# Moving the low-part subtracts of an attention and expert kernel from GpSimd to VectorE

## The chip, the cores and the metric

The kernel runs on one core of a Trainium2 chip. A core has TensorE (PE, matrix multiplies and transposes), VectorE (DVE), ScalarE (ACT), GpSimd (POOL) and a queue engine that only issues transfers (SyncE, SP). Each engine works through its own row of instructions in order, and waits on semaphores for the others. The metric is the device time of one execution in microseconds (us); lower is better.

## The reference, cut to what matters

```python
scores = q @ k.T / sqrt(64) + bias          # 4 batches x 8 heads, 576 x 576
attn = softmax(scores)                      # bias: a small network of the distance
x = (attn @ v) gathered to 2304 x 512
h = x @ w_in                                # 512 x 2048
g = h * tanh(log(1 + exp(h)))               # "mish"
out = g @ w_out                             # 2048 x 512
```

All in float32. The kernel multiplies in a rounded float32 format (F32R) and keeps accuracy by splitting an operand into a high part (the rounded value) and a low part (what the rounding left, value minus high part): three products, high by high, low by high and high by low, stand for one.

## The kernel before, in words

Three stages follow one another. The first (to about 55 us) makes the bias of all heads and writes it to DRAM. The second, attention, works through 16 pairs of heads (4 head pairs times 4 batches). The third is the expert part: two matrix multiplies with the gate between them.

A pair of heads in attention is five steps, one for each block of 128 query rows in the order `ORDER = [0, 1, 4, 2, 3]`; block 4 holds the last 64 rows of both heads, so that step has one score tile and the other four have two. `step(n)` writes a step out by hand, and its order is the order on every engine:

- `scores(n)` (L204): PE multiplies q and k, high and low parts, into score tiles `s`. There are two buffers of `s`, one for each head of a step.
- `add_bias(n)` (L216, one instruction pair at L227 for each head): DVE adds the bias from PSUM into `pt` and takes the row's extreme `m`. This frees `s`.
- `exps(n, 0)` and later `exps(n, 1)` (L232): ACT exponentials of the two heads.
- `transposes(n - 2)` (L272): PE transposes the weights of two steps ago into `tp`, ACT copies them out (`main`, `tail`, L286 to L305). In the second step of a pair the reciprocals of the sums go through here too, and DVE copies them out as `rt` (L254) once ACT has copied `tail`.
- `ahead(n)` (L362): issues loads for later pairs: `load_hi` on POOL's queue (the transfer that rounds to F32R), `load_raw` on SP's (the unrounded q and k, then v).
- `split(n)` (L381): `split_qk` makes the low part `qklo` of the next pair, and one of four parts of a weight's conversion runs: `scale_high`, `shift_low`, `merge`, then `sign` with `split_weights`. A weight so takes four steps, and 16 of them are converted in attention. `split_weights` lets ACT cast the weight to its high part (`whi` or `who`, L143), and an engine given as an argument subtracts (`wli` or `wlo`, L144).
- `pv_duo` (L307): PE multiplies weights and values into the only `o` buffer, in pieces that are spread over steps; DVE copies a finished `o` out as `x` (L325), in the second and fourth step. PE starts the next `o` in the third and fifth step, behind the transposes.

In the prediction steps are called first to fifth: block 0, 1, 4, 2, 3.

Of the kernel before, what the change touches and what calls it, by code (L numbers as in the profile page):

```python
# [7 lines left out]
F32 = mybir.dt.float32  # L8
F32R = mybir.dt.float32r
U32 = mybir.dt.uint32  # L10
AF = mybir.ActivationFunctionType
ALU = mybir.AluOpType
# [3 lines left out]
B, H, S, D, C = 4, 8, 576, 64, 32  # L16
# [3 lines left out]
P = 128  # L20
SH = S // 2
QW = 1280
# [22 lines left out]
def kernel(ctx: ExitStack, tc, qk, v, wb, w2, w_in, w_out, psia, psi4, rinv, eye, out):  # L45
    nc = tc.nc
    pe, dve, act, pool, sp = nc.tensor, nc.vector, nc.scalar, nc.gpsimd, nc.sync
# [57 lines left out]
    def scale_high(eng):  # L105

        job, w = w64.pop(0)
        high = convp.tile([P, 512], F32, name="high", bufs=1)  # L110
        if eng is act:
            act.mul(high, w.bitcast(F32)[:, :, 1], 2.0 ** -112)
        else:
            dve.tensor_scalar(high, w.bitcast(F32)[:, :, 1], 2.0 ** -112, None, op0=ALU.mult)
        half.append((job, w, high))
# [15 lines left out]
    def sign():  # L131
        job, high, c = half.pop(0)
        cu = c.bitcast(U32)
        dve.scalar_tensor_tensor(cu, high.bitcast(U32), 0x80000000, cu,
                                 op0=ALU.bitwise_and, op1=ALU.bitwise_or)
        w32.append((job, c))

    def split_weights(eng):
        job, c = w32.pop(0)
        if job not in w_hi:  # L140
            w_hi[job] = ring.tile([P, 512], F32R, name="wh{}{}{}".format(*job))
            w_lo[job] = ring.tile([P, 512], F32R, name="wl{}{}{}".format(*job))
        act.copy(w_hi[job], c)  # L143
        eng.tensor_tensor(w_lo[job], c, w_hi[job].bitcast(F32), op=ALU.subtract)  # L144
# [11 lines left out]
    hip = rsbuf("hip", 2, side="right")  # L156
# [3 lines left out]
    qk_raw, qk_hi, qk_lo, v_t, bias_t = {}, {}, {}, {}, {}  # L160
    st.tile([P, 32], F32, name="fill", bufs=1)

    def load_raw(i):
        hp, b = divmod(i, B)
        raw = rawp.tile([P, QW], F32, name="rawqk")
        sp.dma_start(out=raw, in_=qk[b, hp])
        vt = vp.tile([P, 2, 5, D], F32, name="vt")
        sp.dma_start(out=vt, in_=v[b, hp].rearrange("p (h c d) -> p h c d", h=2, c=5))
        qk_raw[i], v_t[i] = raw, vt

    def load_hi(i):
        hp, b = divmod(i, B)
        hi = hip.tile([P, QW], F32R, name="qkhi")
        pool.dma_start(out=hi, in_=qk[b, hp])
        qk_hi[i] = hi

    def split_qk(i):

        lo = hip.tile([P, QW], F32R, name="qklo")
        (pool if i else dve).tensor_tensor(lo, qk_raw.pop(i), qk_hi[i].bitcast(F32), op=ALU.subtract)  # L180
        qk_lo[i] = lo

    def load_bias(hp, c):
        h0, h1 = 2 * hp, 2 * hp + 1
        rows = P if c < 4 else 64
        src = bias_d[c][:, :rows * PITCH].rearrange("h (i j) -> h i j", j=PITCH)[:, :, PAD:PAD + S]
        t = bias_t[hp, c] = biasp.tile([P, 2 * S if c < 4 else 640], F32, name=f"bias{c}")[:, :2 * S if c < 4 else S]
        if c < 4:
            sp.dma_start(out=t[:, 0:S], in_=src[h0])
            sp.dma_start(out=t[:, S + 64:], in_=src[h1, :, 0:512])  # L190
            sp.dma_start(out=t[:, S:S + 64], in_=src[h1, :, 512:S])
        else:
            for r in range(2):
                sp.dma_start(out=t[r * 64:r * 64 + 64], in_=src[h0 + r])

    NPAIR = B * HP
# [141 lines left out]
    def load_x(blk, p):  # L338
        t0, n = blocks[blk]
        raw = p.tile([P, HP, TB], F32, name="xraw", bufs=1)  # L340
        for off, m, b, s in _x_runs(t0, n):
            sp.dma_start(out=raw[:, :, off:off + m], in_=x_d[b][:, :, s:s + m])
        x_raw[blk] = raw

    def load_r(blk, r, h0, h1):

        t0, n = blocks[blk]
        for off, m, b, s in _x_runs(t0, n):
            while m:
                k = min(m, 512 - s) if s < 512 else m  # L350
                for u in range(2):
                    if s < 512:
                        src = r_d[b][h0:h1, 4 * u:4 * u + 4].rearrange("p c j -> p (c j)")[:, s:s + k]
                    else:
                        src = r_d[b][h0:h1, 8, 64 * u + s - 512:64 * u + s - 512 + k]
                    sp.dma_start(out=r[64 * u:64 * u + 64, :, off:off + k],
                                 in_=src.unsqueeze(0).to_broadcast([64, h1 - h0, k]))
                off, m, s = off + k, m - k, s + k

    parts = []  # L360

    def ahead(n):  # L362

        i, x = divmod(n, 5)
        if x == 4 and i + 2 < NPAIR:
            load_hi(i + 2)
            load_raw(i + 2)
        if i % B == B - 1 and i // B + 1 < HP:
            load_bias(i // B + 1, ORDER[x])
        if n == NS - 11:  # L370
            load_x(0, x0)
        if n in (NS - 10, NS - 6):
            x_r[0] = x0.tile([P, 2, TB], F32, name="xr", bufs=1)
            h0 = 0 if n == NS - 10 else 2
            load_r(0, x_r[0], h0, h0 + 2)
        if n in (NS - 7, NS - 3):
            h0 = 0 if n == NS - 7 else 2
            for d in range(2):
                pool.tensor_tensor(x_raw[0][:, h0 + d], x_raw[0][:, h0 + d], x_r[0][:, d], op=ALU.mult)

    def split(n):  # L381

        i, x = divmod(n, 5)
        if (x == 1 or n == 3) and i + 1 < NPAIR:
            split_qk(i + 1)
        if half:
            parts.pop(0)()
        elif n > 5 and w64[0][0] in order[:HALF]:
            scale_high(act if x == 2 else dve)
            parts.extend((shift_low, merge, lambda: (sign(), split_weights(pool))))  # L390

    def step(n):
        i, x = divmod(n, 5)
# [63 lines left out]
    def reach(t):  # L457

        left, right = 16 * t + 15, S - 16 * t
        n = max(left + 1, right)  # L460
        return left, right, n + n % 2
# [12 lines left out]
    for idx in range(NB + 2):  # L474
# [4 lines left out]
        if idx + 2 < NB:  # L479
            n = reach(ts[idx + 2])[2]  # L480
# [6 lines left out]
    def make_h(idx):  # L487
        if idx >= NB:
            return
        n = reach(ts[idx])[2]  # L490
        for cg in range(4):
            e = maker[idx, cg]
            ht = ring.tile([P, 640], F32, name="ht")
            k = 4 * ts[idx] + cg
            if e == "a":
                act.activation(ht[:, :n], at[:, :n], AF.Relu, bias=bb[:, k:k + 1])
            else:
                dve.tensor_scalar(ht[:, :n], at[:, :n], bb[:, k:k + 1], 0.0, op0=ALU.add, op1=ALU.max)
            h_t[idx, cg] = ht

    def mirrored(idx):
        t = ts[idx]
        left, right, _ = reach(t)
        ps = bps_t[idx] = bps.tile([P, 1024], F32, name="bps")
        for a, b in ((0, min(left, 512)), (512, left), (left, 512), (max(left, 512), NW)):
            for cg in range(4 if a < b else 0):
                h = h_t[idx, cg]
                src = h[:, a - left:b - left] if a >= left else h[:, left - a:left - b:-1]
                pe.matmul(ps[cg * 32:cg * 32 + 32, a:b], w2t, src, start=True, stop=True)  # L509

    def evac(idx):
        t = ts[idx]
        bt = bo.tile([P, NW], F32, name="bt")
        if maker["out", idx] == "a":
            act.mul(bt, bps_t.pop(idx)[:, :NW], rinv_t[:, t:t + 1])
        else:
            dve.tensor_scalar(bt, bps_t.pop(idx)[:, :NW], rinv_t[:, t:t + 1], None, op0=ALU.mult)

        c = t // 8
        a = (16 * t - P * c) * PITCH + PAD - 15  # L520
        dst = bias_d[c][:, a:a + 16 * (PITCH + 1)].rearrange("h (i j) -> i h j", j=PITCH + 1)
        sp.dma_start(out=dst[:, :, :NW], in_=bt)
# [5 lines left out]
    for idx in range(NB + 2):  # L528
        if idx < NB:
            make_h(idx + 2)  # L530
            mirrored(idx)
        if 1 <= idx <= NB:
            evac(idx - 1)
        if idx == 1:
            load_raw(0)
        if idx == 12:
            split_qk(0)
        if idx in BIAS_AT:
            load_bias(0, ORDER[BIAS_AT.index(idx)])
        for lag, do in enumerate((scores, add_bias, exps)):  # L540
            if idx - lag in SOFT_AT:
                for u in range(2 if lag == 2 else 1):
                    do(SOFT_AT.index(idx - lag), *((u,) if lag == 2 else ()))
        if idx == 33:
            load_hi(1)
        if idx == NB:
            load_raw(1)
        if idx == NB + 1:
            load_weights()
    bias_scope.close()  # L550
# [259 lines left out]
```

## Time and profile before

| | |
|---|---|
| median of 3 runs | 738.5 us (737.0 to 747.25) |
| the profiled execution | 732.05 us, span 730.3 us |
| PE busy | 696.7 us (95%) |
| DVE busy | 507.3 us (69%) |
| ACT busy | 467.3 us (64%) |
| POOL busy | 82.7 us (11%) |

The profiled execution is a single one, and it is 6.5 us below the median of the runs. A busy share is a mean over the three stages. A row of a timeline gives the start in us, the time it was busy, the engine, the line, the operation with output and inputs, and in brackets how long the engine had stood idle before it and what ended the idle time. An operation's busy time overlaps the next one's start by some 0.06 us.

### The profile page before, as it was taken

To read this page: it belongs to the slowest core of one execution; us is meant where nothing else is said; L and a number is where in the kernel's file an instruction comes from. 1 tells how busy PE (TensorE), PEld (TensorE's weight loads), DVE (VectorE), ACT (ScalarE), POOL (GpSimd) and SP (SyncE) were. 2 spreads that over 40 slices of the span, in tenths; PEclk is the share of its full clock that TensorE was granted. 3 is DMA by queue.
4 is the path that set the end of the run, shared out by engine and by line. 5 is a ranking of instruction groups with operands and counts; after the bars stand their busy time and mean duration, and the time that the engine had idled before them with its cause. 6 is when DMAs were issued, how large, how long until landed. Compare 5 with 4: busy or idle time off the path is not lost.

```text
span 730.3 us, 13013 instructions
## 1 busy us (share of the span) xinstructions
PE 696.7 (95%) x4880; PEld 531.5 (73%) x4880; DVE 507.3 (69%) x1020; ACT 467.3 (64%) x964; POOL 82.7 (11%) x57
## 2 busy tenths in 40 slices
PE   6997999999989999989999999999999999999997
PEld 3456766666656666756787888888988888888886
DVE  7884776767667667546888888876676567665564
ACT  7985878888878788864655655654554455454443
POOL 0001324323223224300000000000100000000000
PEclk9999999999999999999999999999999999999999
DMA  7889467448545855341123222024113000010001
GB/s 228 280 270 322 139 197 256 147 154 263 202 144 180 254 204 199 95 132 42 54 59 118 93 78 72 32 100 115 59 63 82 1 0 1 0 59 1 0 1 58
DMA packets 46431, 86.86 MB, mean 119 GB/s; under 512 B 13200, under 2 KB 22048, under 8 KB 46368
## 3 DMA queue, kind: packets, MB, share of 16 engines
q1 hardware_dynamic: 43488, 75.32, 32.5%
q0 software_dynamic: 2304, 10.49, 4.1%
q8 instruction: 38, 0.62, 0.4%
q10 hardware_dynamic: 576, 0.22, 0.1%
q14 instruction: 25, 0.20, 0.1%
HBM read 64.56 MB, written 21.45 MB: 118 GB/s over the span
## 4 chain that ended last, share of the span: by engine, by line
PE 77%; DVE 9%; ACT 8%; issue 3%; DMA 3%; SPq 0%; DVEq 0%; ACTq 0%
PE y L654 24%; PE h L609 23%; PE o L318 9%; PE s L213 9%; PE tp L285 5%; PE bps L509 5%; ACT pt L242 2%; ACT main L286 2%; PE o L322 1%; PE tp L298 1%; DVE w L127 1%; DVE pt L227 1%; DVE e L632 1%; DMA xlo<-r_d 1%; DVE e L616 1%
## 5 line engine op out<-in xcount | busy, mean ns | idle before, releaser
L227 DVE CUSTOM_DVE_ANT_0 pt<-s,bias 128x576 f32<-128x576 f32 x144 | 103.8, 753 | 59.0 <-PE s L213 53.8
L242 ACT ACTIVATE pt<-pt,m 128x576 f32<-128x576 f32 x144 | 112.7, 783 | 49.2 <-DVE m L227 48.0
L654 PE MATMUL y<-who,ghi 128*128 128x512 f32 x288 | 112.5, 391 | 2.2 <-ACT ghi L633 1.4
L654 PE MATMUL y<-who,glo 128*128 128x512 f32 x288 | 112.4, 390 | 1.1 <-DVE glo L636 1.0
L633 ACT CAST ghi<-e 128x512 fp32r<-128x512 f32 x72 | 44.7, 621 | 106.0 <-DVE e L632 101.1
L654 PE MATMUL y<-wlo,ghi 128*128 128x512 f32 x288 | 112.2, 390 | 0.0
L318 PE MATMUL o<-main,vt 128*64 128x320 f32 (+1 forms) x512 | 75.8, 418 | 11.4 <-DVE x L325 11.4
L609 PE MATMUL h<-xhi,whi 128*128 128x512 f32 (+1 forms) x320 | 79.7, 369 | 1.3 <-ACT xhi L584 1.2
L636 DVE TENSOR_TENSOR glo<-e,ghi 128x512 fp32r<-128x512 f32 x72 | 49.7, 691 | 42.1 <-ACT ghi L633 42.1
L609 PE MATMUL h<-xhi,wli 128*128 128x512 f32 (+1 forms) x320 | 78.7, 368 | 0.0
L609 PE MATMUL h<-xlo,whi 128*128 128x512 f32 (+1 forms) x320 | 78.7, 368 | 0.0
L285 PE MATMUL tp<-ident,pt 128*128 128x128 f32 x512 | 70.1, 281 | 1.2 <-ACT main L286 1.2
L614 ACT ACTIVATE e<-h 128x512 f32<-128x512 f32 x72 | 42.7, 593 | 44.1 <-PE h L609 44.1
L615 DVE TENSOR_SCALAR e<-e 128x512 f32<-128x512 f32 x72 | 30.6, 425 | 54.1 <-ACT e L614 54.1
L286 ACT COPY main<-tp 128x512 f32<-128x512 f32 x126 | 66.9, 581 | 1.0 <-PE tp L285 0.6
L609 PEld LDWEIGHTS h<-xhi,whi 128*128 128x128 f32 x320 | 57.3, 188 | 13.5 <-ACT xhi L584 2.7
L654 PEld LDWEIGHTS y<-who,ghi 128*128 128x128 f32 x288 | 54.1, 188 | 14.3 <-ACT ghi L633 2.2
L609 PEld LDWEIGHTS h<-xhi,wli 128*128 128x128 f32 x320 | 56.9, 189 | 10.0
L609 PEld LDWEIGHTS h<-xlo,whi 128*128 128x128 f32 x320 | 56.9, 189 | 10.0
L654 PEld LDWEIGHTS y<-who,glo 128*128 128x128 f32 x288 | 54.1, 188 | 13.6 <-DVE glo L636 2.4
L285 PEld LDWEIGHTS tp<-ident,pt 128*128 128x128 f32 x512 | 56.5, 142 | 10.1 <-ACT tail L292 3.3
L654 PEld LDWEIGHTS y<-wlo,ghi 128*128 128x128 f32 x288 | 54.1, 188 | 10.9
(76 smaller groups left out, 1073.7 us busy)
## 6 DMA issues: line engine op xcount, KB each, us to landing
bias_d<-bt SPq DMA_DIRECT2D x36, 295.5 KB
qkhi<-in_qk_dram POOLq DMA_DIRECT2D x16, 640.0 KB, 7.0
rawqk<-in_qk_dram SPq DMA_DIRECT2D x16, 640.0 KB
w<-in_w_in_dram SPq DMA_DIRECT2D x16, 512.0 KB
w<-in_w_out_dram SPq DMA_DIRECT2D x16, 512.0 KB
vt<-in_v_dram SPq DMA_DIRECT2D x16, 320.0 KB
bias<-bias_d SPq DMA_DIRECT2D x16, 288.0 KB
out_dram<-w SPq DMA_DIRECT2D x17, 256.0 KB
```

Of the source, the lines that this page charges most:

```text
L213: pe.matmul(live[n][h][:, j, :SH], stat[rows, c * P:(c + 1) * P], mov[rows, k0:k0 + SH], start=(k == 0), stop=(k == 2))
L227: dve.tensor_tensor_reduce(out=halves(pt[:, sl]), in0=s[:, :, :SH], in1=halves(bt[:, sl]), scale=-0.125, scalar=BIG, op0=ALU.add, op1=ALU. ...
L242: act.activation(ps, ps, AF.Exp, bias=m[:, u:u + 1], scale=-1.0, accum_out=sums[i][:, k:k + 1])
L285: pe.transpose(tp[:, k * P:(k + 1) * P], pt[:, c0:c0 + P], ident)
L286: (dve.tensor_copy if n < 2 and h else act.copy)(main[:, h, :, off:off + P], tp.rearrange("p (k q) -> p k q", k=4))
L318: pe.matmul(o[h * 64:h * 64 + 64, :w], vt[:, h, k, :], main[:, h, k, :], start=(k == 0), stop=False, **kw)
L509: pe.matmul(ps[cg * 32:cg * 32 + 32, a:b], w2t, src, start=True, stop=True)
L609: pe.matmul(h[:, u * n:(u + 1) * n], w["i", g4, d][:, r * P:(r + 1) * P], x[:, d, :n], start=(k == 0), stop=(k == 11))
L614: act.activation(e, h, AF.Exp)
L633: act.copy(ghi, e)
L636: dve.tensor_tensor(glo, e, ghi.bitcast(F32), op=ALU.subtract)
L654: pe.matmul(ys[blk][t], g[:, c0:c0 + P], w, start=((blk, f) in first and k == 0), stop=((blk, f) in last and k == 2))
```

## The change

All subtracts that make low parts in attention go from POOL to DVE: the 15 that make `qklo` for q and k of both heads (the first pair's was there already), and the 16 of the weights. `split_qk` moves from the second to the third step of a pair. The high parts `qkhi` have three buffers and not two, and `load_hi` and `load_raw` for the pair after the next are issued in the second step of a pair and not in the fifth (except in the first pair); the load of v is taken out of `load_raw` and stays in the fifth.

```diff
     def load_hi(i):
         hp, b = divmod(i, B)
-        hi = hip.tile([P, QW], F32R, name="qkhi")
+        hi = hip.tile([P, QW], F32R, name="qkhi", bufs=3)
         pool.dma_start(out=hi, in_=qk[b, hp])
         qk_hi[i] = hi
 
     def split_qk(i):
 
         lo = hip.tile([P, QW], F32R, name="qklo")
-        (pool if i else dve).tensor_tensor(lo, qk_raw.pop(i), qk_hi[i].bitcast(F32), op=ALU.subtract)
+        dve.tensor_tensor(lo, qk_raw.pop(i), qk_hi[i].bitcast(F32), op=ALU.subtract)
         qk_lo[i] = lo
...
         i, x = divmod(n, 5)
-        if x == 4 and i + 2 < NPAIR:
+        if x == (1 if i else 4) and i + 2 < NPAIR:
             load_hi(i + 2)
             load_raw(i + 2)
+        if x == 4 and i + 2 < NPAIR:
+            load_v(i + 2)
...
         i, x = divmod(n, 5)
-        if (x == 1 or n == 3) and i + 1 < NPAIR:
+        if (x == 2 or n == 3) and i + 1 < NPAIR:
             split_qk(i + 1)
         if half:
             parts.pop(0)()
         elif n > 5 and w64[0][0] in order[:HALF]:
             scale_high(act if x == 2 else dve)
-            parts.extend((shift_low, merge, lambda: (sign(), split_weights(pool))))
+            parts.extend((shift_low, merge, lambda: (sign(), split_weights(dve))))
```

On DVE, in the fourth step of the third pair, where a weight's conversion ends (`pt,m` is the bias operation of a head, the lone `m` its read of the extreme, `w_1559` the weight, `x` the copy of `o`), the row before is:

```order
L227 ISA pt,m<-s,bias_966 128x576
L227 ISA m 128x1
L134 SCALAR_TENSOR_TENSOR w_1559<-high,w_1559 128x512
L325 COPY x<-o 128x320
L227 ISA pt,m<-s,bias_1093 128x576
```

and with the change:

```order
L231 ISA pt,m<-s,bias_966 128x576
L231 ISA m 128x1
L134 SCALAR_TENSOR_TENSOR w_1563<-high,w_1563 128x512
L144 TENSOR_TENSOR wli_120<-w_1563,whi_119 128x512
L329 COPY x<-o 128x320
```

The subtract `wli`, whose input `whi` comes from ACT, now stands between `sign` and the copy `x`.

On DVE again, at the border of the second and third step of the same pair, the row before is:

```order
L254 COPY rt<-tp 9x128
L120 TENSOR_SCALAR low<-w_1100 128x512
L325 COPY x<-o 128x256
L227 ISA pt_1539,m<-s,bias_799 128x576
L227 ISA m 128x1
L127 SCALAR_TENSOR_TENSOR w_1559<-high,low 128x512
L227 ISA pt,m<-s,bias_966 128x576
```

and with the change:

```order
L258 COPY rt<-tp 9x128
L120 TENSOR_SCALAR low<-w_1100 128x512
L329 COPY x<-o 128x256
L231 ISA pt_1541,m<-s,bias_799 128x576
L231 ISA m 128x1
L184 TENSOR_TENSOR qklo<-rawqk,qkhi 128x1280
L127 SCALAR_TENSOR_TENSOR w_1563<-high,low 128x512
L231 ISA pt,m<-s,bias_966 128x576
```

The operation for `qklo` stands between the third step's one bias operation and its weight part.

On POOL, from the end of its set-up, the row before is:

```order
L174 DMA qkhi<-in_qk_dram 128x1280 x2
L180 ISA
L180 TENSOR_TENSOR qklo<-rawqk,qkhi 128x1280
L174 DMA qkhi<-in_qk_dram 128x1280
L180 TENSOR_TENSOR qklo<-rawqk,qkhi 128x1280
L174 DMA qkhi<-in_qk_dram 128x1280
L144 TENSOR_TENSOR wli_118<-w_1380,whi_117 128x512
```

and with the change:

```order
L814 UNCONDITIONAL_BRANCH
L178 DMA qkhi<-in_qk_dram 128x1280 x16
L385 ISA
L385 TENSOR_TENSOR xraw<-xraw,xr 128x512 x4
L691 TENSOR_TENSOR w_6048<-w_6324,w_6048 128x512
```

Between the loads of `qkhi` nothing else is left on POOL until the end of attention.

## Rows read from the trace of the kernel before

**Rows 1.** Timeline of PE, 92 to 110 us: start, busy, instruction, idle before
```profile
92.53 1.84 PE L318 MATMUL o<-main,vt 128*64 128x320 f32 x12 [0.74 <-DVE x L325]
94.29 0.53 PE L213 MATMUL s<-qkhi 64*128 64x288 f32 x4
...
97.64 0.53 PE L213 MATMUL s<-qkhi 64*128 64x288 f32 x4
...
100.45 0.53 PE L213 MATMUL s<-qkhi 64*128 64x288 f32 x4
...
103.59 0.53 PE L213 MATMUL s<-qkhi 64*128 64x288 f32 x4
...
108.84 1.84 PE L318 MATMUL o<-main,vt 128*64 128x320 f32 x12 [0.39 <-DVE x L325]
```

**Rows 2.** Waits of PE and DVE, 60 to 300 us: total us, times, longest us
```profile
PE o L318 <- DVE x L325: 10.5, 12, 2.5
...
DVE rt L254 <- ACT tail L292: 21.0, 14, 1.7
```

**Rows 3.** Timelines of POOL, DVE and PE around 206 to 212 us
```profile
206.42 2.89 POOL L180 TENSOR_TENSOR qklo<-rawqk,qkhi 128x1280 fp32r<-128x1280 f32 x1 [0.21 <-DMA qkhi<-in_qk_dram]
...
206.98 2.62 DVE L114 TENSOR_SCALAR high<-w 128x512 f32<-128x512 f32 x1
...
209.99 1.84 PE L318 MATMUL o<-main,vt 128*64 128x320 f32 x12 [2.51 <-DVE x L325]
```

**Rows 4.** By tile and line, whole span: count, ns min/median/max, first and last start
```profile
L180 DVE TENSOR_TENSOR qklo<-rawqk,qkhi x1: 1485/1485/1485, 21.5 to 21.5; 128x1280 fp32r<-128x1280 f32 x1
...
L144 DVE TENSOR_TENSOR wli<-w,whi x8: 691/693/694, 333.9 to 408.6; 128x512 fp32r<-128x512 f32 x8
```

**Rows 5.** Timelines of DVE and ACT, a fourth step with `sign`
```profile
96.74 0.69 DVE L134 SCALAR_TENSOR_TENSOR w<-high,w 128x512 uint32<-128x512 uint32 x1
97.76 0.49 DVE L325 COPY x<-o 128x320 f32<-128x320 f32 x1 [0.33 <-PE o L322]
98.73 0.76 DVE L227 CUSTOM_DVE_ANT_0 pt<-s,bias 128x576 f32<-128x576 f32 x1 [0.48 <-PE s L213]
...
98.89 0.62 ACT L143 CAST whi<-w 128x512 fp32r<-128x512 f32 x1
```

**Rows 6.** Timelines of DVE and ACT, a fifth step with `sign`
```profile
83.42 0.69 DVE L134 SCALAR_TENSOR_TENSOR w<-high,w 128x512 uint32<-128x512 uint32 x1
85.00 0.76 DVE L227 CUSTOM_DVE_ANT_0 pt<-s,bias 128x576 f32<-128x576 f32 x1 [0.89 <-PE s L213]
...
85.39 0.60 ACT L143 CAST whi<-w 128x512 fp32r<-128x512 f32 x1
```

**Rows 7.** Timelines of DVE and ACT, a first step with `sign`
```profile
202.27 0.63 DVE L134 SCALAR_TENSOR_TENSOR w<-high,w 128x512 uint32<-128x512 uint32 x1
203.71 0.76 DVE L227 CUSTOM_DVE_ANT_0 pt<-s,bias 128x576 f32<-128x576 f32 x1 [0.81 <-PE s L213]
...
204.22 0.63 ACT L143 CAST who<-w 128x512 fp32r<-128x512 f32 x1
```

**Rows 8.** Timelines of DVE and ACT, a second step with `sign`
```profile
124.69 0.41 DVE L325 COPY x<-o 128x256 f32<-128x256 f32 x1
...
124.80 0.62 ACT L143 CAST whi<-w 128x512 fp32r<-128x512 f32 x1 [0.18 <-DVE w L134]
```

**Rows 9.** Timelines of PE, ACT and DVE, a third step with `sign`
```profile
243.76 1.84 PE L318 MATMUL o<-main,vt 128*64 128x320 f32 x12 [1.49 <-DVE x L325]
...
246.29 0.64 ACT L143 CAST who<-w 128x512 fp32r<-128x512 f32 x1
...
246.62 0.76 DVE L227 CUSTOM_DVE_ANT_0 pt<-s,bias 128x576 f32<-128x576 f32 x1 [1.64 <-PE s L213]
```

**Rows 10.** Timeline of PE at the stage's start, and its granted clock there
```profile
66.84 0.40 PE L213 MATMUL s<-qkhi 64*128 64x288 f32 x1 [1.78 <-DVE m L227]
...
70.00:72.00 2.00, 2.00 (x14) 0.51 1.04 412
```

More of the change, by code (lines that the diff above doesn't have):

```diff
@@ L166, in load_raw, with load_v @@
         sp.dma_start(out=raw, in_=qk[b, hp])
+        qk_raw[i] = raw
+    def load_v(i):
+        hp, b = divmod(i, B)
         vt = vp.tile([P, 2, 5, D], F32, name="vt")
         sp.dma_start(out=vt, in_=v[b, hp].rearrange("p (h c d) -> p h c d", h=2, c=5))
-        qk_raw[i], v_t[i] = raw, vt
+        v_t[i] = vt
     def load_hi(i):
         hp, b = divmod(i, B)
-        hi = hip.tile([P, QW], F32R, name="qkhi")
+        hi = hip.tile([P, QW], F32R, name="qkhi", bufs=3)
         pool.dma_start(out=hi, in_=qk[b, hp])
@@ L535 @@
             load_raw(0)
+            load_v(0)
         if idx == 12:
@@ L547 @@
             load_raw(1)
+            load_v(1)
         if idx == NB + 1:
```

## The prediction

> **What bounds the kernel now.** I read first, in the timeline, what TensorE (PE) does in the attention stage, step by step. A pair of heads is five steps; I call them first to fifth. From one third step's `o` matmuls to the next, 92.53 to 108.84, is 16.31 us, and PE stands still in it only for the 0.39 us ahead of the second `o` [rows 1]. So this stage is bound by PE's own row of instructions, and a time on another engine matters only where PE waits for it. The table of waits says where that is: `o` waits for VectorE's (DVE's) copy `x`, 10.5 us in 12 waits, the longest 2.5 [rows 2]. Nothing the change does can give back more than those 10.5 us, 1.4% of the profile's 732.05 us. Behind the attention stage PE is full again, so a shift there arrives at the end in full.
>
> Why that copy is late is told by two facts. The small copy `rt` in front of it waits in 14 pairs for ScalarE (ACT), 21.0 us in all [rows 2]: this part comes back whatever GpSimd (POOL) does. And where POOL runs its subtract for `qklo`, 206.42 to 209.31, the DVE operation begun at 206.98 takes 2.62 us and ends only behind it, after which PE has waited 2.51 us [rows 3]. The reader is to see both: an ordinary wait of about 0.39 us that stays, and a collision on top in some pairs.
>
> **What the change removes.** All 31 subtracts leave POOL (15 `qklo`, 16 weights), so the collisions go. Had each of the 12 waits been an ordinary one of 0.39, they would hold 12 x 0.39 = 4.7 us; the collisions are worth 10.5 - 4.7 = 5.8 us.
>
> **What it adds: qklo on DVE.** Such an operation took 1.49 us there [rows 4]. It is in the third step, which has one bias operation where others have two. DVE's row from `x` on: bias 0.75, `qklo` 1.49, a weight operation of at most 0.69 [rows 5], 2.9 us. The fourth step's bias operation starts 2.86 us behind `o` (243.76 to 246.62) [rows 9]. It just fits: I take 0. Without that room it would cost up to 15 x 0.7 = 10 us.
>
> **What it adds: a wait for ScalarE inside DVE's row.** This is the term that decides. A weight's last part is `sign` on DVE, a cast on ACT, then the subtract. On POOL the subtract waited aside. Now it stands right behind `sign` in DVE's row (first order piece), and what is queued behind it there, the bias operations, `x` and `rt`, waits too. ACT takes the cast after the step's two exponentials and its copies, so it comes late. There are 16 such jobs, one every four steps, so they fall on the fifth step four times and on each other step three times. The subtract is 0.69 us [rows 4], and I allow 0.06 us for the signal. PE's next scores need the buffers that the bias operations free. In a step of length L the slack is L - 1.09 (97.64 scores to 98.73 bias [rows 1, 5]) - 2 x 0.75 [rows 5].
>
> *Fourth step:* the cast ends at 98.89 + 0.62 = 99.51, the subtract at 100.26, the `x` copy (0.49, less 0.06 overlap) at 100.69; the next bias operation stood at 98.73 [rows 5]. Late by about 1.95; the fifth step is 2.81 long (97.64 to 100.45 [rows 1]), slack 0.22: PE loses 1.7. Three times: 5.1.
>
> *Fifth step:* the cast ends 85.99, the subtract 86.74 against 85.00 [rows 6]: late by 1.7. The first step is 3.14 long (100.45 to 103.59 [rows 1]), slack 0.55: at least 1.15. But ACT's exponentials start 1.7 late too, and `rt`, then `x`, then `o` hang on them [rows 2]. I take 1.6 between 1.15 and 1.7. Four times: 6.4.
>
> *First step:* the cast ends 204.85, the subtract 205.6 against 203.71 [rows 7]: late by 1.9, and two steps before `o`, so again through ACT and `rt`. Since the third step's scores need only one of two buffers, a head's time (0.75) or more may be hidden: between 0.9 and 1.9, and I take 1.8, since the ACT copies for `rt` follow that exponential without a gap. Three times: 5.4.
>
> *Second step:* the `x` copy that started at 124.69 has to wait for the cast's end, 125.42, and the subtract, 126.17 [rows 8]: 1.45 late, with no slack, three times: 4.4.
>
> *Third step:* with `qklo` in front, `sign` ends 2.75 behind `o`; ACT comes to the cast 2.53 behind it (243.76 to 246.29) [rows 9], so it ends at 3.4 and the subtract at 4.1 against 2.86: late by 1.25. The fourth step is 3.35 long (94.29 to 97.64 [rows 1]), slack 0.76: 0.5, three times: 1.5.
>
> Sum 22.8 us. The losses of first and fifth step are counted at `o` with its ordinary wait in them; six pairs more (jobs in second and third step) keep their 0.39, 2.3 us. All waits after: 25.1 against 10.5 before, +14.6 us.
>
> **The loads.** A third `qkhi` buffer lets POOL issue each load as soon as a buffer is free, and `rawqk` is issued three steps earlier while it is wanted one step later than before. POOL waited for `qkhi` before (0.21 at 206.42 [rows 3]); now the lead is longer than a pair, so I price it at 0. It also stands on SP's queue before `r_d` and the weights' load instead of behind `x_d`; the cover is that lead of more than 16 us [rows 1]. At the stage's start `qklo` of the second pair goes into DVE's row ahead of an `x` and a bias operation; that bias operation was the one PE waited 1.78 us for [rows 10]. Between 0 and 1.49, I take 0.3, since DVE has little else to do there.
>
> **The sum.** 14.6 + 0.3 = 14.9 us on the profiled execution's 732.05: 746.9. The median of the runs shown is 738.5, 6.5 above it; the steps are the same there, so I forecast 738.5 + 14.9 = 753. That is +2.0%; 2% (14.8 us) is about what a measurement of this kernel can tell from no change.
>
> **The rivals.**
>
> *Not slower: the port freed is worth what the waits cost.* For it: the DVE operation of rows 3 lost 2.2 us to POOL, so part of the time that POOL saved was paid by DVE anyway, and DVE has idle time in every step (0.48 at 98.73 [rows 5], more elsewhere). If PE only lost the direct part in the fifth and first step, 4 x 0.7 + 3 x 0.5 (deeper buffers than I see), half in the fourth and second, 3 x 0.85 + 3 x 0.7, and nothing in the third, losses are 9, the six ordinary waits 2.3, together 11.3 against 10.5: no change, 739. It decides if a cast comes 1 us earlier than in rows 5 to 7. Against it: ACT's row ahead of the cast is not touched. The Trainium skill (Perfetto Trace Analysis, Optimizing Scalar/DVE Operations) says that moving work between GpSimd and VectorE might not help because they share an SBUF port. By that rule alone, bringing the work back costs little and this rival would hold; rows 3 agree with the sharing, but not rows 5 to 7, where the cost is a wait for a third engine. Chance 0.16; of it 0.03 that it even ends more than 2% faster, for which more than all 10.5 us would have to come back.
>
> *Slower still: PE's clock falls in the new gaps.* After the idle at 66 us the granted clock was 0.51, the lower level, from 70 to 72 us [rows 10], and matmuls took longer. Against it: the 2.51 us gap before 209.99 left the 12 matmuls at the 1.84 us that they have elsewhere [rows 1, 3]. If three pairs, those with two jobs each, lost 2 us so, or `qklo` waited for its loads as much, it is +21, 760. Chance 0.22.
>
> *My forecast:* chance 0.62. Its bounds: all lower ends (1.15 and 0.9, third step 0, start 0) give 5.1 + 4.6 + 2.7 + 4.4 + 2.3 - 10.5 = +8.6; all upper ends with the start at 1.49 give 5.1 + 6.8 + 5.7 + 4.4 + 3.8 + 2.3 - 10.5 + 1.5 = +19. Its own range is 747 to 758. The 2% line lies in its middle, so it gives half to each side.
>
> Together: faster 0.03, same 0.13 + 0.31 = 0.44, slower 0.31 + 0.22 = 0.53. For 8 in 10 I go from 742, into the first rival, to 764, beyond the second.
>
> **What would show it.** Right: in the changed profile `sign` is followed on DVE by an idle of 0.6 to 2.1 us that ends with ACT's cast, 16 times, some 23 us (by rows 5 to 9 about 2.1, 1.9, 2.0, 0.7 and 0.7 on fourth, fifth, first, second and third step); no weight operation above 0.8 us in the stage; PE waits for `m` of the bias operations in fourth and fifth step jobs, and for `x` in the others, 25 us in all; `qklo` at 1.49 without idle before it. Wrong: PE's waits stay under 15 us (the slack or the cast is not where I read it), `qklo` waits for a DMA, or the granted clock dips behind 75 us.

## The result, and the profile after

The changed kernel takes 743.54 us in the median of 20 runs (742.32 to 746.58), the kernel before 741.53 us in 20 runs (732.51 to 749.56). The ratio is 1.0059, with a 95% interval of 1.0038 to 1.0081: 0.6% slower, within what counts as the same at 2%. (The ratios here and below leave out runs more than 1.5% above the fastest of their kernel, so they are not the quotients of the medians.) The forecast was 753 us, 2.0% slower.

The two spreads differ more than the medians. The runs of the kernel before lie within 17 us, those of the changed kernel within 4. And the profile on which the prediction was built, 732.05 us, turned out to lie below every one of the 20 runs of the kernel before. The profiled execution of the changed kernel took 745.56 us, 13.5 us more than that; the sum in the prediction was +14.9.

Waits of PE after the change, 60 to 300 us (total us, times, longest us):

```profile
PE o L322 <- DVE x L329: 12.0, 15, 1.8
PE s L217 <- DVE m L231: 6.5, 11, 1.6
PE tp L289 <- ACT main L290: 1.1, 3, 0.4
```

Against [rows 2] the wait for the copy `x` is a little longer, and that for the bias operations' `m`, 2.2 us in 2 waits before, has grown to 6.5 in 11. The waits of DVE in the same window say where both come from:

```profile
DVE rt L258 <- ACT tail L296: 19.7, 13, 1.8
DVE wlo L144 <- ACT who L143: 13.2, 8, 2.1
DVE wli L144 <- ACT whi L143: 10.8, 8, 2.1
...
DVE qklo L184 <- DMA rawqk<-in_qk_dram: 2.8, 1, 2.8
```

DVE stands idle for ACT's cast in all 16 weight jobs, 24.0 us together. For `qklo` it waited for a transfer once, at the start of the stage; at no later pair did a load come late. A fourth step with `sign`, in the timelines of DVE, ACT and PE, answers to [rows 5]:

```profile
168.13 0.69 DVE L134 SCALAR_TENSOR_TENSOR w<-high,w 128x512 uint32<-128x512 uint32 x1
170.93 0.69 DVE L144 TENSOR_TENSOR wli<-w,whi 128x512 fp32r<-128x512 f32 x1 [2.11 <-ACT whi L143]
171.54 0.48 DVE L329 COPY x<-o 128x320 f32<-128x320 f32 x1
...
170.28 0.62 ACT L143 CAST whi<-w 128x512 fp32r<-128x512 f32 x1
...
172.08 1.08 PE L322 MATMUL o<-main,vt 128*64 128x256 f32 x8 [1.19 <-DVE x L329]
```

`sign` ends at 168.82, the cast at 170.90, and behind them the subtract, `x` and PE's `o` follow one after the other. The collisions are gone. The groups of DVE's weight operations by line (count, busy us and mean ns) are, 60 to 300 us:

```profile
L127 DVE SCALAR_TENSOR_TENSOR w<-high,low 128x512 uint32<-128x512 uint32 x16 | 10.7, 671 | 0.0
L134 DVE SCALAR_TENSOR_TENSOR w<-high,w 128x512 uint32<-128x512 uint32 x16 | 10.7, 671 | 0.0
L120 DVE TENSOR_SCALAR low<-w 128x512 uint32<-128x512 uint32 x16 | 6.5, 406 | 0.0
```

None of them is stretched to the 2.62 us of [rows 3] any more; the longest takes 0.69.

### The profile page after: what moved, and what is told of

Its sections match the earlier page's. It is cut to its first block, busy times and chain, and to the rows that moved or that the text cites. A ratio compares the mean times of both kernels' runs of the same rounds, so it can differ in the third digit from the quotient of the medians.

```text
span 743.6 us, 12982 instructions
## 1 busy us (share of the span) xinstructions
PE 703.2 (95%) x4880; PEld 534.3 (72%) x4880; DVE 516.1 (69%) x1051; ACT 466.9 (63%) x964; POOL 16.5 (2%) x26
## 4 chain that ended last, share of the span: by engine, by line
PE 73%; ACT 11%; DVE 10%; issue 3%; DMA 2%; SPq 0%; DVEq 0%; ACTq 0%
PE y L662 23%; PE h L617 22%; PE s L217 8%; PE o L322 8%; PE tp L289 5%; PE bps L515 4%; ACT pt L246 4%; ACT main L290 2%; DVE pt L231 2%; PE o L326 1%; DMA xlo<-r_d 1%; DVE x L329 1%; DMA rawqk<-in_qk_dram 1%; ACT whi L143 1%; DVE e L640 1%
## 5 line engine op out<-in xcount | busy, mean ns | idle before, releaser
L322 PE MATMUL o<-main,vt 128*64 128x320 f32 (+1 forms) x512 | 75.8, 418 | 12.9 <-DVE x L329 12.9
L617 PEld LDWEIGHTS h<-xhi,whi 128*128 128x128 f32 x320 | 57.3, 188 | 13.5 <-ACT xhi L592 2.7
```

The costliest lines, as they stand in the source:

```text
L322: pe.matmul(o[h * 64:h * 64 + 64, :w], vt[:, h, k, :], main[:, h, k, :], start=(k == 0), stop=False, **kw)
L617: pe.matmul(h[:, u * n:(u + 1) * n], w["i", g4, d][:, r * P:(r + 1) * P], x[:, d, :n], start=(k == 0), stop=(k == 11))
```

## The experiments

Two theories were put against each other. A: the change costs what the prediction worked out, but a typical execution of the kernel before loses more to POOL's collisions than the profiled one, so the change also gives back more. B: the time above the profile lies elsewhere, and the waits for the cast cost less than worked out.

| kernel | median us | ratio to the kernel before, 95% interval |
|---|---|---|
| the change | 743.54 | 1.0059 (1.0038 to 1.0081) |
| e1: weights' subtracts back on POOL | 724.54 | 0.9765 (0.9693 to 0.9836) |
| e2: before, weights' subtracts on DVE alone | 756.9 | 1.0221 (1.0122 to 1.0319) |
| e3: the change, weights' subtracts a step later | 723.51 | 0.9758 (0.9684 to 0.9832) |
| e4: e3, and `x` ahead of the weight operation | 718.81 | 0.9664 (0.9615 to 0.9713) |
| e5: before, third buffer and early loads alone | 745.03 | 1.0014 (0.9982 to 1.0046) |
| e6: e3 with `qklo` in the second step | 743.25 | 1.0014 (0.9977 to 1.0051) |
| e7: e3 with two `qkhi` buffers | 723.41 | 0.9722 (0.9663 to 0.9782) |
| e8: before, POOL's `qklo` held behind `x` | 725.11 | 0.9745 (0.9698 to 0.9792) |

The intervals of e1, e2 and e3 contain 2%: it is shown that these kernels differ from the kernel before, and not that they do so by 2%. The kernel before ran beside each group again, with medians of 744.04 (e0 to e3), 742.56 (e4 to e7) and 743.21 us (e8, e9); the gains below are against these.

**e0 and e9: the kernel before, profiled again.** No edit.

> The kernel before once more, for a second profile of it: its 20 runs spread from 732.5 to 749.6 us, and the profile that the prediction read is one of 732.05. Theory A (the time that a typical execution has above that profile is POOL's collisions with DVE, which vary with the landing of the loads): a profile of 738 us or more shows PE waiting for the copy x for 15 to 20 us between 60 and 300 us, where the first profile had 10.5, and the other stages as long as before. Rival B (the extra time lies in the bias stage or the expert part, and the change did not touch it): PE's waits in attention stay at 10 to 11 us, and the first or third stage is longer by the difference.

> The kernel before a third time, for a third profile beside 732.05 and 742.13 us. Theory A: PE's wait for x between 60 and 300 us goes with the time, 10.5 us at 732 and 18.7 at 742, so about 0.8 us of wait for each us of time; the three profiles lie on one line. Rival B: the time and that wait are not tied, the difference lies in the first or third stage.

They took 742.13 and 744.76 us. PE's wait for `x`, 10.5 us in [rows 2], in the two new profiles (first e0, then e9):

```profile
PE o L318 <- DVE x L325: 18.7, 12, 2.7
```

```profile
PE o L318 <- DVE x L325: 17.4, 12, 2.8
```

The attention stage can be cut out between the first pair's `o` matmuls and the first matmul of the expert part. In the timeline of PE these are, for the first profile of before, for e0 and for the change:

```profile
75.86 1.83 PE L318 MATMUL o<-main,vt 128*64 128x320 f32 x12
...
320.76 2.06 PE L609 MATMUL h<-xhi,whi 128*128 128x512 f32 x4 [1.22 <-ACT xhi L584]
```

```profile
74.86 1.84 PE L318 MATMUL o<-main,vt 128*64 128x320 f32 x12
...
330.99 2.06 PE L609 MATMUL h<-xhi,whi 128*128 128x512 f32 x4 [1.22 <-ACT xhi L584]
```

```profile
75.35 1.84 PE L322 MATMUL o<-main,vt 128*64 128x320 f32 x12
...
333.12 2.22 PE L617 MATMUL h<-xhi,whi 128*128 128x512 f32 x4 [1.22 <-ACT xhi L592]
```

That is 244.9, 256.1 and 257.8 us. What is left of the executions is 487.2, 486.0 and 487.8 us, the same within 2. So the whole difference between two executions of the kernel before lies in attention, and in e0 this stage is as long as after the change. B falls. One point of A was too simple: e9 was slower than e0 with a shorter wait for `x`, so the time doesn't go with that wait alone (the last section has more).

Why the same program falls so differently is seen in one pair. In the first profile, POOL, DVE and PE were:

```profile
140.55 3.21 POOL L180 TENSOR_TENSOR qklo<-rawqk,qkhi 128x1280 fp32r<-128x1280 f32 x1 [0.74 <-DMA qkhi<-in_qk_dram]
...
140.59 0.41 DVE L114 TENSOR_SCALAR high<-w 128x512 f32<-128x512 f32 x1
...
141.38 1.84 PE L318 MATMUL o<-main,vt 128*64 128x320 f32 x12 [0.30 <-DVE x L325]
...
141.93 2.12 DVE L120 TENSOR_SCALAR low<-w 128x512 uint32<-128x512 uint32 x1
```

and in e0 the same pair:

```profile
142.58 2.89 POOL L180 TENSOR_TENSOR qklo<-rawqk,qkhi 128x1280 fp32r<-128x1280 f32 x1
...
143.38 2.38 DVE L114 TENSOR_SCALAR high<-w 128x512 f32<-128x512 f32 x1
...
146.14 3.11 PE L318 MATMUL o<-main,vt 128*64 128x320 f32 x12 [2.27 <-DVE x L325]
```

In the first, the two began within 0.04 us, DVE kept its 0.41 us and POOL was stretched to 3.21; in e0 POOL was 0.8 us ahead, and DVE's operation ended at 145.76, 0.29 us behind POOL's end. The Trainium skill (SBUF — State Buffer, Who interferes with whom) says that the order of issue decides which of the two blocks, and that the loser waits out the other's whole instruction. The rows of e0 agree; those of the first profile can't show it, since by its recorded start POOL was 0.04 us ahead there and was still the one stretched. DVE lost time in the first profile too: its next weight operation, `low`, took 2.12 us. But that one stands behind `x`, so PE's `o` had already begun. By tile, POOL's subtracts (count, ns min/median/max) were, in the first profile and in e0:

```profile
L180 POOL TENSOR_TENSOR qklo<-rawqk,qkhi x15: 2894/2927/3622, 64.4 to 290.8; 128x1280 fp32r<-128x1280 f32 x15
```

```profile
L180 POOL TENSOR_TENSOR qklo<-rawqk,qkhi x15: 2882/2904/2995, 63.5 to 301.4; 128x1280 fp32r<-128x1280 f32 x15
```

In the first profile POOL was the one stretched several times (up to 3.62), in e0 never by more than 0.1. Counted in PE's timeline, waits of over 1.4 us for `x` came in four pairs of the first profile, in eight of e0 and in seven of e9. The prediction's profile was an execution in which the collision seldom fell ahead of `x`.

**e1: the weights' subtracts back on POOL.**

```diff
-            parts.extend((shift_low, merge, lambda: (sign(), split_weights(dve))))
+            parts.extend((shift_low, merge, lambda: (sign(), split_weights(pool))))
```

> The changed kernel with one part undone: the 16 subtracts of the weights are on POOL again, qklo stays on DVE. The 24 us in which DVE stands idle for ACT's cast go, and short collisions (1.28 us on POOL each) come back. Theory A: PE's waits in attention fall from about 20 to 6 to 9 us, the time to 729 to 734 us, and the runs lie within 4 us of each other, since no collision with qklo is left. Rival B (the waits for the cast are mostly slack, so undoing them gives little): 740 to 744 us.

724.54 us, faster than theory A gave. So `qklo` on DVE in the third step, with the loads, is worth 19.5 us against the 744.04 us that the kernel before took beside it (17 by the ratio of the table), and the weights' move costs 743.54 - 724.54 = 19.0 us. PE's waits were:

```profile
PE o L322 <- DVE x L329: 3.4, 9, 0.6
...
PE s L217 <- DVE m L231: 1.2, 2, 0.9
```

No wait for `m` is left behind the stage's start, so `qklo` in the third step costs PE nothing.

**e2: the kernel before with the weights' subtracts on DVE alone.** The edit is `split_weights(pool)` to `split_weights(dve)`.

> The kernel before with one part of the change alone: the 16 subtracts of the weights go to DVE, qklo and the loads stay as they were. Theory A: the waits for the cast cost their 12 to 15 us on top of the collisions: 750 to 757 us, and the wide spread of the kernel before stays. Rival B: 741 to 745 us, as the whole change measured.

756.9 us, within A's range: 756.9 - 744.04 = 12.9 us by the medians, 2.2% (16 us) by the ratio. Here the collisions and the waits for the cast stand in one profile:

```profile
PE o L318 <- DVE x L325: 18.9, 14, 3.7
PE s L213 <- DVE m L227: 7.2, 11, 2.1
```

The wide spread that A expected to stay wasn't seen: four runs, 756.1 to 760.56, are too few to say.

**e3: each weight's subtract one step later.** The cast stays where it is; DVE subtracts behind the next step's bias operations.

```diff
+                if subs:
+                    low_weights()
```

(in `begin()` behind `add_bias(n)`; `low_weights` issues the subtract that `split_weights` has put aside.)

> The changed kernel with each weight's subtract put one step later in DVE's row, behind that step's bias operations, by when ACT's cast is done. All the work of the changed kernel is there. Theory A: DVE's idle for the cast (24 us) falls to under 3, PE's waits in attention from about 20 to 5 to 8, the time to 729 to 733 us. Rival B: no gain over the changed kernel, 740 to 744 us.

723.51 us. With the same operations on the same engine as in the change, 20 us are saved by the place of 16 instructions. PE's waits are nearly those of e1: 3.2 us for `x` in 9 waits, and 1.5 for `m` in 2, at the stage's start.

The time is below A's 729: A had subtracted the recorded waits alone, and PE loses more than those, since matmuls behind a wait can be stretched in the record. In the change, a group of four `s` matmuls behind the wait ahead of 172.08 took 0.86 us, where such a group otherwise took 0.53.

**e4: the copy `x` first.** In the second step, `split(n)` is called behind `pv_duo` and not ahead of it.

```diff
-            if n < NS:
+            if n < NS and x != 1:
                 split(n)
...
+        if x == 1 and n < NS:
+            split(n)
```

> The kernel of e3 (every weight's subtract one step later) with one more move: in the second step of a pair the weight operation stands behind the copy x in DVE's row, not in front of it. e3 and e1 still show PE waiting for x 9 times, 3.2 to 3.4 us in all, after merges and signs in front of x. Theory A (those waits are the ordinary ones of 0.39 us that the prediction named): they go, PE's waits between 60 and 300 us fall to about 2 us, the time to 719 to 722 us, 2 to 4 us below e3. Rival B (rt and ACT's copy set the moment, not the weight operation): as e3, 722 to 725 us.

718.81 us (718.77 to 719.05), slightly better than expected and 3.4% below the kernel before. PE's waits, 60 to 300 us, are four, all ahead of the first pair's `o`:

```profile
PE s L226 <- DVE m L240: 1.6, 2, 0.9
PE tp L298 <- ACT main L299: 1.4, 2, 1.0
```

The ordinary waits ahead of `o` were the weight operation in front of `x`: `rt` still waits 15 times for ACT here, 20.6 us in all, and PE waits for none of it. The stage, cut as above, is now bound by PE alone:

```profile
74.49 1.84 PE L331 MATMUL o<-main,vt 128*64 128x320 f32 x12
...
106.20 1.83 PE L331 MATMUL o<-main,vt 128*64 128x320 f32 x12
...
307.98 2.06 PE L630 MATMUL h<-xhi,whi 128*128 128x512 f32 x4 [1.22 <-ACT xhi L605]
```

A pair takes 15.86 us here (74.49 to 106.20 are two). 233.5 us for the stage is the floor against which the other kernels can be read: they are 11.4 us above it in the first profile of before, 22.6 in e0, 24.3 in the change. This version beats both kernels.

**e5: the third buffer and the early loads alone.** The diff of the change without the three edits from `pool` to `dve` and from `x == 1` to `x == 2`.

> The kernel before with the third qkhi buffer and the early loads alone; all subtracts stay on POOL. Theory A (the spread of the kernel before comes from the moment at which a load lands, since that starts POOL's qklo and with it the collision): the subtract no longer waits for a load, so it falls at one fixed place in a pair, and the runs lie within 4 us of each other instead of 12 to 17; where it falls ahead of x the time is 740 to 745 us, where it falls elsewhere 724 to 732. Rival B (the spread has another cause): 735 to 748 us, as wide as before.

745.03 us in 10 runs from 742.94 to 747.28. The spread fell from 15.7 us (19 runs of the kernel before beside it, 736.45 to 752.16) to 4.3, nearly as A expected, with the time at the upper end of A's. From 87 us on the subtract waits for no load any more, but it falls where it hurts. In three pairs that is ahead of `x`:

```profile
143.44 2.90 POOL L184 TENSOR_TENSOR qklo<-rawqk,qkhi 128x1280 fp32r<-128x1280 f32 x1
...
143.68 2.95 DVE L114 TENSOR_SCALAR high<-w 128x512 f32<-128x512 f32 x1
...
147.02 1.84 PE L322 MATMUL o<-main,vt 128*64 128x320 f32 x12 [2.84 <-DVE x L329]
...
158.71 3.52 DVE L114 TENSOR_SCALAR high<-w 128x512 f32<-128x512 f32 x1
...
159.04 2.90 POOL L184 TENSOR_TENSOR qklo<-rawqk,qkhi 128x1280 fp32r<-128x1280 f32 x1
```

The last two rows are a first step, where bias operations wait behind the collision, and PE's next `s` 2.00 us for them; this too comes three times. In all, PE's waits here are 12.7 us for `x` and 9.5 for `m`.

**e6: `qklo` in the second step.** e3 with `x == 2` in `split` set back to `x == 1`.

> The kernel of e3 with qklo on DVE in the second step of a pair, where the subtract stood in the code before, and not in the third. Theory A (the third step has room for 1.5 us of DVE work, the second has none, since x waits behind it): PE waits for x about 1.4 us longer in each of 15 pairs, the time is 20 us above e3: 741 to 746 us. Rival B (DVE has room there too, while it waits for rt): within 4 us of e3.

743.25 us, 19.7 us above e3. PE waits for `x` 20.4 us, in 12 pairs. Here POOL has none of these subtracts left, and the kernel is still no faster than the kernel before (1.0014): with `qklo` in the second step, freeing POOL gains nothing. The gain of e1 and e3 is in the place.

**e7: two buffers of `qkhi`.** e3 without `bufs=3`.

> The kernel of e3 with two buffers of qkhi as before, the early place of the loads in the code kept. The load then has to wait for the scores of the pair before the last, so it starts at a pair's end and lands 6 to 8 us later, about when the third step's qklo is due. Theory A (the buffer is what makes the load early): DVE waits for qkhi in several pairs, 0.3 to 1 us each, the time is 2 to 10 us above e3, 726 to 734 us, with more spread. Rival B (the load is early enough with two): as e3, 722 to 726 us.

723.41 us, as e3. Theory A missed here: DVE waited for `qkhi` in no pair. The third buffer, with `qklo` on DVE's third step, is worth nothing that could be measured.

**e8: POOL keeps everything, but starts behind `x`.** From the third pair on:

```diff
+        if after is not None:
+            pool.tensor_copy(st.tile([P, 1], F32, name="gate", bufs=2), after[:, 0:1])
```

where `after` is the tile of the copy `x`; `split_qk` is called behind that copy.

> The kernel before with all subtracts left on POOL, but from the third pair on POOL first copies one column of the copy x of the second step into a spare tile, so that its subtract for qklo starts behind x whenever the load landed. Nothing else is moved. Theory A (what costs is the moment of the collision: ahead of x PE waits for it, behind x the third step's slack hides it): PE's waits for x fall to 4 to 7 us, the time to 724 to 731 us, and the runs lie within 4 us. Rival B (any collision costs, wherever it falls, since DVE's lost time is the same): 738 to 748 us, and PE's waits move to the bias operations.

725.11 us (724.46 to 727.9). The collision is still there, in the third step:

```profile
143.63 2.92 POOL L183 TENSOR_TENSOR qklo<-rawqk,qkhi 128x1280 fp32r<-128x1280 f32 x1
...
144.03 2.80 DVE L120 TENSOR_SCALAR low<-w 128x512 uint32<-128x512 uint32 x1
146.75 0.74 DVE L230 CUSTOM_DVE_ANT_0 pt<-s,bias 128x576 f32<-128x576 f32 x1
```

DVE loses as much as ever, 2.4 us, and PE waits for none of it. So what the kernel before paid was not DVE's lost time, but its place ahead of `x`. Nearly the whole gain of `qklo` on DVE was to be had with the subtract left on POOL.

## Why the prediction was wrong

**What bounds the kernel: right.** PE binds attention, and only its waits count. e4, without them, runs at PE's own pace. The bound "Nothing the change does can give back more than those 10.5 us" was wrong as a statement on the kernel: it held for the one execution that was read. e4 gave back 24 us of the median.

**What the change removes: the step that failed.** The collisions were put at 5.8 us, from 12 waits less an ordinary 0.39 each. The ordinary part was right in size: 4.7 us worked out, and e3 still had 4.4 us more in the stage than e4 (312.64 - 74.75 = 237.9 against 233.5). Its reason was not: the prediction laid it to `rt`'s wait for ACT, and e4 shows that it was the weight operation in front of `x`. For the execution that was read, the collisions were nearly right too: 11.4 - 4.4 = 7.0 us against 5.8. For the kernel they were mis-sized. In e0 they are 22.6 - 4.4 = 18.2 us, and e1 gained 17 to 19.5 us. The prediction read their price from one execution in which few of them fell ahead of `x`, and carried it to the median with the words "the steps are the same there". The 6.5 us between the profile and the median, which it saw, were to be looked for in this term: in e0 and e9 the time above the first profile lies in attention, where the collisions are.

**`qklo` on DVE: right.** 1.48 us each, no wait for `m` from it, taken at 0 (e1). e6 shows what the room in the third step hides: 20 us.

**The wait for the cast inside DVE's row: right in mechanism, and nearly in size.** 23 us of idle were forecast, 24.0 came, and by steps 2.1, 1.9, 2.0, 0.7 and 0.7. PE's loss over a floor without waits was put at 25.1 us; it is 24.3. PE's timeline after the change has it pair by pair:

```profile
92.80 1.83 PE L322 MATMUL o<-main,vt 128*64 128x320 f32 x12 [0.33 <-DVE x L329]
...
110.69 1.83 PE L322 MATMUL o<-main,vt 128*64 128x320 f32 x12 [0.38 <-DVE x L329]
...
128.66 1.84 PE L322 MATMUL o<-main,vt 128*64 128x320 f32 x12 [1.76 <-DVE x L329]
...
146.46 1.84 PE L322 MATMUL o<-main,vt 128*64 128x320 f32 x12 [0.34 <-DVE x L329]
```

From 75.35 on these four pairs hold a fifth-step job, a fourth, a third with a second, and a first. By the prediction's terms, with the ordinary 0.39 us that it lets two of them keep, they should lose 1.6, 2.1, 2.3 and 1.8 us; against the 15.86 us of a pair in e4 they lose 1.6, 2.0, 2.1 and 1.9. The recorded waits show less, 1.19 us ahead of `o` for the fourth step's 1.7. There the path was another than forecast: PE waits for `x`, not for `m`. The price of the weights' part alone is 19.0 us by e1, and 13 to 16 by e2; that collisions hide a part of it in e2 is likely, but not shown.

**The loads: right at 0.** No load came late behind the stage's start; e5 shows that they alone change the spread and not the median, e7 that the third buffer isn't needed.

**The sum against one execution: right; against the median: wrong.** 13.5 us came between the two profiled executions, where 14.9 were worked out, and not by luck: the losses were 24.3 us where 25.1 were said, and 11.4 before where 10.5 were read. The median moved by 2 us where 14.5 were forecast. Two moves of about 19 us with opposite signs cancelled in the median.

**The rivals.** "The port freed is worth what the waits cost" is what happened, by its sum, and not by its reason: it assumed that the losses shrink, while the gain was larger. The rule of the Trainium skill beside it (Perfetto Trace Analysis, Optimizing Scalar/DVE Operations: moving work between GpSimd and VectorE might not help, for the shared port) agrees with e6 in the outcome, where `qklo` on DVE in the second step gained nothing, though not in the reason: there the operation itself stands ahead of `x`. In the third step it gained 17 to 19.5 us (e1), left on POOL but held there nearly as much (e8), and what took the gain back was the wait for a third engine. "PE's clock falls in the new gaps" did not happen: around the change's waits in attention, up to 1.8 us, the granted clock stayed 1.00. It was 0.59, near the lower level, once more, from 335 to 339 us, at the start of the expert part behind a wait for ACT, which lies behind the stage.

## What to carry to other kernels

Before a profile is made the base of a sum, see where it stands among the runs: if the spread is wide and the profiled execution lies at one end, take another profile of the same kernel and look for the place of the difference. A subtract that needs another engine's result should not stand in an in-order row right behind the work that feeds that engine: the same 16 instructions one step later were worth 20 us. And ask of a collision not how long it holds an engine, but what waits behind that engine at that moment: moving the work to another engine and moving it to another place are two changes, and here the place was worth nearly all.

## What the runs showed of the hardware

POOL's subtracts and DVE's weight operations held each other up for whole operations (a `high` of 0.41 us took 2.38 in e0 and ended 0.29 us behind POOL's); DVE's bias operations, 0.75 us, and its copies `rt` and `x`, 0.28 and 0.41, kept their lengths beside POOL. The recorded starts don't tell which of the two waits: in e0 the later one did (142.58 and 143.38), in the first profile POOL did though recorded 0.04 us ahead (140.55 and 140.59), and in e5 DVE's `high` did though recorded 0.33 us ahead (158.71 and 159.04). What decides it is left open.

PE's granted clock can fall behind a single gap of that kind. In e0, around the wait of 2.68 us ahead of 218.35, it was (start and end, length, PE busy, granted clock, DMA share, GB/s):

```profile
216.00:218.00 2.00, 0.00 (x0) 1.00 0.01 2
218.00:220.00 2.00, 1.65 (x6) 0.56 0.19 66
220.00:222.00 2.00, 2.00 (x12) 0.59 0.74 252
222.00:224.00 2.00, 2.00 (x23) 1.00 0.03 10
```

For some 4 us it was near the lower of its two levels, 1.2 GHz, and the 12 matmuls took 3.45 us where they take 1.84. Behind the 2.51 us of [rows 3] it did not fall, and behind the 2.84 us of e5 and the 2.67 us ahead of 127.97 in e0 itself neither; in e9 it did behind 1.86 us, ahead of 272.64. So the length of the gap alone doesn't decide it; what does is left open. In e0 the clock fell so behind two gaps, in e9 behind three. One fall cost some 1.6 us in the rows above (3.45 less 1.84), an estimate; e9's stage (75.94 to 333.61) is 1.5 us longer than e0's, which this would explain.
